# Spreading the last token group's block-sum splits over more slots, and moving the sums of the sixth output operand two sevenths ahead

## The chip, the cores and the metric

The kernel runs on one core of a Trainium2 chip. The metric is the device time of one execution in microseconds (us). TensorE (PE in the profile) multiplies matrices; VectorE (DVE), ScalarE (ACT) and GpSimd (POOL) do the elementwise work; SyncE (SP) issues the DMAs. Each engine works through its own instruction list in order, and waits on semaphores where an instruction needs another engine's result.

## What is computed

Causal attention over 4 batches of 12 heads (448 tokens, head size 64) gives `x` of 1792 tokens by 768. A gated feed-forward block follows:

```
rms  = sqrt(mean(x*x, axis=-1) + 1e-6)
xn   = x / rms * rms_g
g    = xn @ w_gate                       # 768 -> 1536
val  = xn @ w_val
out  = (g / (1 + exp(-g)) * val) @ w_out # 1536 -> 768
```

## The kernel before

**Precision.** Every float32 operand of the feed-forward products is split into a rounded high part (cast on ACT) and a low part (the difference, on DVE or POOL). A product is then three matmuls: high by high, high by low, low by high. So each operand costs one ACT cast, and behind it one subtraction on DVE or POOL.

**Stages.** The tokens form three groups: two of 512 and a last one of 768. The two groups of 512 go through the feed-forward in two passes over 36 weight units each (24 of gate and value, 12 of output weights; two units make one output block). A unit is three *slots* of six matmuls each; slot n of the second pass is the (n mod 3)-th part of unit (n-1)//3, so unit 33 takes slots 100 to 102. The attention work is interleaved with these passes. The third group's gate and value product, and its output product, come last. Both are done as a 2 by 2 block product with seven products in place of eight (a Winograd form), which needs sums and differences of blocks of both operands.

**The order around the first edit.** Everything is emitted in program order by one loop over slots, so every engine's queue holds the work in slot order. `split_w(s + 3)` (L384) is called in the last slot of each unit: it casts the weights of a unit three ahead on ACT (`w_h`, L389), and two slots later their low part `w_l` is subtracted, on DVE (L391) for odd units of the output weights and on POOL (L393, helper L102) for even ones. `ffn_part` (L421) emits the matmuls (L435 to L437; the third of each trio needs `w_l`) and, at the end of an output block, the eviction `ob` on DVE (L443), whose store SP issues three slots later (L445). The output block's PSUM bank is one of two with the tag "m". The loads of weight units (L361) and of the next stage's operands (`quad_load`, L560) are in SP's queue among these stores.

Once the attention is done (after slot 74 of the second pass), `x_steps` (L483) returns the list `todo`, and each later slot runs one entry of it. It scales the third group's `x` (L514), forms the block sums `t1`, `t2`, `t4` of three column chunks c on DVE (`sums`, L525, by `sub`, L523), and splits operand i, chunk c (`operand`, L535, which calls `split`, L472): one cast on ACT (L473), and a subtraction `cl`, on POOL for i in 0, 2 and 5, on DVE (L475) for 1, 3, 4 and 6. Twelve entries bring the scales and four early operands, three more the sums with one operand each; the last four entries hold all of operands 1, 3, 4 and 6, with (2, 2) and (5, 2) among them: slots 90, 91, 92 and 93.

**The order around the second edit.** The output product runs q = 0 to 20, with i, p = divmod(q, 3): seventh i, token chunk p (L939 to L950). After the 18 matmuls of step q the loop emits: the split of a weight operand of the next seventh (`wo_split`, cast `a_h` on ACT, `a_l` on DVE; six buffers), the load of one for the seventh after it (`wo_load`, SP, L661), the eviction (`out_result`, DVE, L717), for i = 0 sums and for i = 2 a difference on DVE, and then `h_operand(q + 4)` (L684), which casts the hidden operand `oh` on ACT and subtracts `ol` (on POOL for p = 0, else on DVE). There are four buffers of `oh` and `ol`, so the cast for step q + 4 can't start before step q's matmuls are through. For the sixth operand (i = 5, q + 4 = 15 to 17), `h_operand` first forms the difference `a12 - s2` on DVE (L692), and the cast behind it on ACT reads that. Each `out_product` of seventh i reads the three weight operands 3i to 3i + 2 in turn, six matmuls for each.

Of the kernel before, what the change touches and what calls it, by code (L numbers as in the profile page):

```python
# [14 lines left out]
ALU = mybir.AluOpType  # L15
# [46 lines left out]
def attention_ffn(ctx: ExitStack, tc: tile.TileContext, qk0, qk1, qk2, v, v2, w, g, out, out2):  # L62
# [7 lines left out]
    nc = tc.nc  # L70
# [22 lines left out]
    def bank(tag, bufs=1):  # L93


        return ps.tile([P, W], F32, tag=tag, name=tag + "_ps", bufs=bufs)
# [33 lines left out]
    def post(delay, fn):  # L130
        if delay <= 0:
            fn()
        else:
            later.setdefault(now[0] + delay, []).append(fn)
# [337 lines left out]
    def split(h, l, src, vec):  # L472
        nc.scalar.copy(h, src)  # L473
        if vec:
            nc.vector.tensor_tensor(l, src, f32(h), op=ALU.subtract)  # L475
        else:
            pool_op(l, src, ALU.subtract, f32(h))
# [5 lines left out]
    def x_steps():  # L483

        sm = side["sm"]
        rc = sm.tile([P, 6], F32, name="rc")
        dg = sm.tile([P, 2, HX], F32, tag="p2", name="dg").rearrange("p a (b c) -> p (a b) c", c=P)
        rb = {}

        def columns():  # L490
            ps = bank("t")[:, :6]
            for i in range(6):
                nc.tensor.matmul(ps[:, i: i + 1], acc[2, i // 3][:, P * (i % 3): P * (i % 3 + 1)],
                                 ones[:, :1], start=True, stop=True)
            nc.scalar.activation(rc, ps, AF.Sqrt, bias=eps, scale=1.0 / DM)
            post(1, lambda: nc.vector.reciprocal(rc, rc))

        def diagonal():
            for i in range(6):
                r = rc[:, i: i + 1]  # L500
                if i % 2:
                    nc.scalar.mul(dg[:, i], ident, r)
                else:
                    nc.gpsimd.tensor_scalar(dg[:, i], ident, r, 1.0, op0=ALU.mult, op1=ALU.mult)

        def spread():
            for j in (0, 1):
                rb[j] = bank("xy"[j])[:, :HX]
                nc.tensor.matmul(rb[j], ones, dg[:, 3 * j: 3 * j + 3].rearrange("p a b -> p (a b)"),
                                 start=True, stop=True)  # L510

        def scale(c, j):
            x = xr[2, c][:, HX * j: HX * (j + 1)]
            nc.vector.scalar_tensor_tensor(  # L514
                out=x, in0=x, scalar=g_sb[:, c: c + 1], in1=rb[j], op0=ALU.mult, op1=ALU.mult)

        tmp = {}

        def blk(k, j, c):
            return xq[c][:, k, HX * j: HX * (j + 1)]  # L520

        def sub(dst, a, b):
            nc.vector.tensor_tensor(dst, a, b, op=ALU.subtract)  # L523

        def sums(c):  # L525
            t12 = sm.tile([P, 2, HX], F32, tag=f"p{c}", name="t12")
            t1, t2 = t12[:, 0], t12[:, 1]
            t4 = sm.tile([P, HX], F32, tag=f"t4{c}", name="t4")
            sub(t1, blk(0, 1, c), blk(0, 0, c))
            sub(t2, blk(1, 1, c), t1)  # L530
            sub(blk(0, 1, c), blk(1, 1, c), blk(0, 1, c))
            sub(t4, blk(1, 0, c), t2)
            tmp[c] = t1, t2, t4

        def operand(i, c):  # L535
            if i not in xc:
                xc[i] = tuple(side["xc"].tile([P, 3, HX], F32R, name=f"{n}{i}") for n in ("ch", "cl"))
            t1, t2, t4 = tmp.get(c, (None,) * 3)
            src = (blk(0, 0, c), t2, blk(1, 0, c), t1, blk(0, 1, c), blk(1, 1, c), t4)[i]
            split(xc[i][0][:, c], xc[i][1][:, c], src, i not in (0, 2, 5))  # L540

        def scales(q):
            return [lambda j=j: scale(q, j) for j in (0, 1)]

        def op(i, c):
            return [lambda: operand(i, c)]

        todo = [[columns], [], [diagonal], [], [spread], [], scales(0), scales(3),
                scales(1) + op(0, 0), scales(4) + op(2, 0), scales(2) + op(5, 0), scales(5) + op(0, 1)]
        for c, i, k in ((0, 2, 1), (1, 5, 1), (2, 0, 2)):  # L550
            todo.append([lambda c=c: sums(c)] + op(i, k))
        for i, x in ((1, op(2, 2)), (3, op(5, 2)), (4, []), (6, [])):
            todo.append(op(i, 0) + op(i, 1) + op(i, 2) + x)
        return todo


# [1 line left out]
    f2 = {}  # L558
# [96 lines left out]
    def wo_load(n):  # L655
        if n >= 21:
            return
        i, sl = divmod(n, 3)
        t = wr_p.tile([P, 2, 3, P], F32, tag="w", name="w_o")
        for m in range(3):  # L660
            nc.sync.dma_start(out=t[:, :, m], in_=WSRC[i](m).rearrange("p (k m) -> p k m", m=P)[  # L661
                :, 2 * sl: 2 * sl + 2])
        wt["o", n] = t

    def wo_split(n):
        if n >= 21:
            return
        f2["o", n] = ring(8 * NF // 2 + n)
        split(*f2["o", n], wt["o", n].rearrange("p a b c -> p (a b c)"), True)

    def h_part(p):
        return [hid[:, 6 * k: 6 * k + 6, HX * e + P * p: HX * e + P * (p + 1)] for e in (0, 1) for k in (0, 1)]

    def h_sums(p):
        a11, _, a21, a22 = h_part(p)
        s1, s2 = f2["s", p] = [side["s"].tile([P, 6, P], F32, tag=n, name=n, bufs=3) for n in ("s1", "s2")]
        nc.vector.tensor_tensor(s1, a21, a22, op=ALU.add)
        nc.vector.tensor_tensor(s2, s1, a11, op=ALU.subtract)

    def h_difference(p):  # L680
        a11, _, a21, _ = h_part(p)
        nc.vector.tensor_tensor(a21, a11, a21, op=ALU.subtract)

    def h_operand(q):  # L684

        if q >= 21:
            return
        i, p = divmod(q, 3)
        a11, a12, a21, a22 = h_part(p)
        s1, s2 = f2.get(("s", p), (None, None))  # L690
        if i == 5:
            nc.vector.tensor_tensor(a12, a12, s2, op=ALU.subtract)  # L692
        src = (a11, a12, s2, s1, a21, a12, a22)[i]
        h, l = (side["ro" if q else "ro0"].tile([P, 6, P], F32R, tag=n, name=n) for n in ("oh", "ol"))
        split(h, l, src, p or not q)
        f2["h", q] = h, l

    def out_product(i, p):
        if i in (0, 4):
            f2["held", p] = bank("mmx"[p], 2 if p < 2 else 1)[:, :HX]  # L700
        ps = f2["held", p] if i in (0, 1, 4, 6) else bank("s", 2)[:, :HX]
        h = f2.pop(("h", 3 * i + p))
        for k in range(6):
            b = [t[:, HX * (k % 2): HX * (k % 2 + 1)] for t in f2["o", 3 * i + k // 2]]
            seven(ps, [t[:, k] for t in h], b, k == 0 and i not in (1, 6), k == 5)
        return ps

    def out_result(i, p, ps):

        g_ = side["g"]  # L710

        def add(n, u, bufs):
            t = g_.tile([P, HX], F32, tag=n, name=n, bufs=bufs)
            if u is None:
                nc.scalar.mul(t, ps, 0.5)
            else:
                nc.vector.scalar_tensor_tensor(out=t, in0=ps, scalar=0.5, in1=f2[u, p], op0=ALU.mult, op1=ALU.add)  # L717
            f2[n, p] = t
            return t

        if i in (0, 2, 3):
            add(*(("m1", None, 3), 0, ("u2", "m1", 3), ("u4", "u2", 3))[i])
            return
        c = add("c", {1: None, 4: "u4", 5: "u4", 6: "u2"}[i], 3)
        e, n = {1: (0, 0), 4: (1, 1), 5: (0, 1), 6: (1, 0)}[i]
        t0 = HX * e + P * p
        nc.sync.dma_start(out=out2[t0: t0 + P, HX * n: HX * (n + 1)], in_=c)
# [55 lines left out]
    with tc.manual_schedule():  # L783
# [32 lines left out]
        n = 0  # L816
        for t_, s, c in early:
            n = max(n, t_)
# [22 lines left out]
        todo = None  # L841
        for s in range(2 * NU):
# [9 lines left out]
            n = s + 6 - 2 * NU  # L852
# [5 lines left out]
            for k0 in (0, 2, 4):  # L858
# [3 lines left out]
                i = 3 * (s % NU) + k0 // 2 + 1  # L862
# [14 lines left out]
                n = 3 * (s - 2 * NU + 2) + k0 // 2  # L877
# [5 lines left out]
                if todo is None and done == len(steps) and i >= AT[1] + 1:  # L883
# [5 lines left out]
                    todo = x_steps()  # L889
# [14 lines left out]
        for v in range(NF):  # L904
            if v % 3 == 1 and v < 9:
                wo_sums(v // 3)
            for i in range(7):
                ps_ = quad_product(v, i)
                quad_result(v, i, ps_)
                if v + 1 < NF:  # L910
                    n = (0, 1, None, 2, None, 3, None)[i]
# [7 lines left out]
                if v + 2 < NF:  # L919
                    n = (None, None, 0, 1, None, 2, 3)[i]  # L920
# [13 lines left out]
        for q in range(1, 4):  # L934
            h_operand(q)
# [3 lines left out]
        for q in range(21):  # L939
            i, p = divmod(q, 3)  # L940
            ps_ = out_product(i, p)
            if i:
                wo_split(3 * (i + 1) + p)
                wo_load(3 * (i + 2) + p)
            out_result(i, p, ps_)
            if i == 0:
                h_sums(p)
            elif i == 2:
                h_difference(p)
            h_operand(q + 4)  # L950


# [46 lines left out]
```

## Time and profile before

| | us |
|---|---|
| median of three runs | 700.14 |
| lowest, highest | 699.67, 701.06 |
| the profiled execution | 702.16 |
| its span, first to last instruction | 700.40 |
| PE busy in it | 671.0 (96%) |
| DVE, ACT, POOL busy | 536.9, 371.6, 361.9 |

The profiled execution is 1.76 us longer than its span, and 2.02 us longer than the median of the runs. Times in the rows below count from the start of the span. A row of a timeline has the start in us, the duration in us, the engine, the line of the kernel, the operation, the tiles written and read, the shape, and a count; where an engine sat idle before the instruction, brackets give for how long and what ended the wait.

### The profile page before, as it was taken

What the parts mean: (1) busy time and instruction counts of PE and PEld (TensorE: products, weight loads), DVE (VectorE), ACT (ScalarE), POOL (GpSimd) and SP (SyncE); (2) the same over time, 40 slices, a digit from 0 to 9 for tenths busy, and PEclk for the clock granted to TensorE, in tenths of its full rate; (3) what the DMA queues carried; (4) which work ended last, traced back from release to release, by engine and by line L of the source; (5) the groups of instructions that cost most, each with busy time, mean ns of one, the idle gap of its engine ahead of it and who ended that gap; (6) DMA issues with size and microseconds to landing.
All of it is one profiled execution on the core that took longest, in us unless ns stands there. A gap on an engine that the chain in (4) does not pass through costs nothing. (4 is left out here: it accounts for less than half of the span.)

```text
span 700.4 us, 11930 instructions
## 1 busy us (share of the span) xinstructions
PE 671.0 (96%) x4106; PEld 550.9 (79%) x4106; DVE 536.9 (77%) x1029; ACT 371.6 (53%) x832; POOL 361.9 (52%) x313
## 2 busy tenths in 40 slices
PE   9878889999999999999999999997999999999997
PEld 6445667777777768777777777886999999999987
DVE  4976899989997667777687877396386868679973
ACT  6967876777685435436445353451433342445540
POOL 4988445545548534665776565552363536302220
PEclk9999999999999999999999999998999999999999
DMA  8746486868778547576767655333567576562541
GB/s 267 259 146 205 146 281 222 281 232 277 233 280 302 193 117 263 164 258 194 251 190 237 212 155 177 118 120 109 162 204 250 177 246 223 168 165 86 171 119 67
DMA packets 71355, 138.80 MB, mean 198 GB/s; under 512 B 7744, under 2 KB 39232, under 8 KB 71296
## 3 DMA queue, kind: packets, MB, share of 16 engines
q1 hardware_dynamic: 71296, 138.05, 60.3%
q8 instruction: 32, 0.52, 0.3%
q14 instruction: 27, 0.22, 0.1%
HBM read 104.21 MB, written 33.82 MB: 197 GB/s over the span
## 5 line engine op out<-in xcount | busy, mean ns | idle before, releaser
L208 POOL TENSOR_SCALAR sp<-sp,rs 128x384 f32<-128x384 f32 (+3 forms) x132 | 89.5, 696 | 95.8 <-DVE rs L212 84.8
L435 PE MATMUL m_ps<-xh,w_h 128*128 128x512 f32 x282 | 120.2, 426 | 3.7 <-DVE rs L212 3.7
L203 ACT ACTIVATE sp<-sp,nm 128x384 f32<-128x384 f32 (+3 forms) x168 | 87.2, 522 | 47.7 <-DVE nm L200 47.1
L437 PE MATMUL m_ps<-xh,w_l 128*128 128x512 f32 x282 | 111.3, 395 | 0.0
L436 PE MATMUL m_ps<-xl,w_h 128*128 128x512 f32 x282 | 111.1, 394 | 0.0
L102 POOL TENSOR_TENSOR a_l<-w_q,a_h 128x768 fp32r<-128x768 f32 x24 | 47.4, 1977 | 75.7 <-ACT a_h L473 75.6
L375 POOL TENSOR_SCALAR w<-w 128x768 f32<-128x768 f32 x36 | 46.5, 1292 | 53.1 <-ACT w_c L374 47.0
L274 PEld LDWEIGHTS a_ps<-pt,v_r 128*64 128x64 f32 (+1 forms) x864 | 40.7, 137 | 36.2 <-issue 11.1
L274 PE MATMUL a_ps<-pt,v_r 128*64 128x128 f32 (+2 forms) x864 | 57.1, 268 | 9.7 <-DVE pt L252 7.3
L435 PEld LDWEIGHTS m_ps<-xh,w_h 128*128 128x128 f32 x282 | 53.3, 189 | 16.1 <-issue 8.0
L437 PEld LDWEIGHTS m_ps<-xh,w_l 128*128 128x128 f32 x282 | 53.4, 189 | 12.1
L252 DVE COPY pt<-t_ps 128x384 f32<-128x384 f32 (+1 forms) x71 | 42.5, 598 | 26.6 <-PE t_ps L248 26.4
L437 PE MATMUL m_ps<-hh,w_l 128*128 128x512 f32 x144 | 57.8, 401 | 4.3 <-DVE w_l L391 3.9
L102 POOL TENSOR_TENSOR w_l<-w_r,w_h 128x768 fp32r<-128x768 f32 x30 | 59.2, 1979 | 3.6 <-ACT w_h L389 3.4
L436 PEld LDWEIGHTS m_ps<-xl,w_h 128*128 128x128 f32 x282 | 53.6, 190 | 7.8
L435 PE MATMUL m_ps<-hh,w_h 128*128 128x512 f32 x144 | 59.2, 411 | 0.0
L200 DVE CUSTOM_DVE_ANT_0 sp<-s_ps,mask 128x128 f32<-128x128 f32 (+3 forms) x136 | 49.8, 415 | 11.1 <-PE s_ps L191 9.3
L436 PE MATMUL m_ps<-hl,w_h 128*128 128x512 f32 x144 | 57.1, 397 | 0.0
L248 PE MATMUL t_ps<-ident,sp 128*128 128x128 f32 (+1 forms) x309 | 50.9, 277 | 1.4 <-ACT rms L335 0.8
L377 DVE SCALAR_TENSOR_TENSOR w<-w 128x768 int32<-128x768 int32 x36 | 45.4, 1261 | 8.0 <-POOL w L375 8.0
L248 PEld LDWEIGHTS t_ps<-ident,sp 128*128 128x128 f32 (+1 forms) x309 | 38.1, 138 | 16.7 <-POOL sp L208 2.6
L473 ACT CAST a_h<-w_q 128x768 fp32r<-128x768 f32 (+1 forms) x48 | 35.0, 753 | 24.9 <-PE m_ps L436 19.1
(176 smaller groups left out, 1702.1 us busy)
## 6 DMA issues: line engine op xcount, KB each, us to landing
w<-in_w SPq DMA_DIRECT2D x36, 768.0 KB, 5.9
w<-w_c SPq DMA_DIRECT2D x36, 384.0 KB, 2.7
w_r<-w SPq DMA_DIRECT2D x36, 384.0 KB, 4.5
qk_r<-in_qk SPq DMA_DIRECT2D x48, 256.0 KB, 4.0
qk_r<-in_qk SPq DMA_DIRECT2D x12, 512.0 KB, 5.6
v_r<-in_v SPq DMA_DIRECT2D x12, 448.0 KB, 5.1
v_r<-in_v SPq DMA_DIRECT2D x24, 192.0 KB, 3.4
wy<-w_r SPq DMA_DIRECT2D x24, 192.0 KB, 4.9
```

Source lines behind the costliest of these rows:

```text
L102: nc.gpsimd.tensor_tensor(out_, a, b, op=op)
L200: nc.vector.tensor_tensor_reduce(out=sp, in0=ps, in1=mk, scale=nsc, scalar=3.0e38, op0=ALU.add, op1=ALU.min, accum_out=nm)
L203: post(T["exp" if p >= ENDS[0] else "exp0"], lambda: nc.scalar.activation(sp, sp, AF.Exp, bias=nm, scale=-1.0, accum_out=sm))
L208: pr["norms"].append(lambda: nc.gpsimd.tensor_scalar(sp, sp, rs, 1.0, op0=ALU.mult, op1=ALU.mult))
L248: nc.tensor.transpose(ps[:kb, at: at + P], pr["sp"][e][:, o + kb * j: o + kb * (j + 1)], ident)
L252: nc.vector.tensor_copy(pt[:kb, :at], ps[:kb, :at])
L274: nc.tensor.matmul(av_ps[e * D: (e + 1) * D, p % 2, q0: q0 + n], raw_v[p][:kb, h, j, e, :], pr["pt", e][:kb, a0: a0 + n], start=(j == 0), ...
L375: (T["c1"], lambda: nc.gpsimd.tensor_scalar(hf_, hf_, 0.0, 1.0, op0=ALU.mult, op1=ALU.mult)),
L377: (T["c2" if s >= 5 else "c20"], lambda: nc.vector.scalar_tensor_tensor(out=lo, in0=lo, scalar=29, in1=hi, op0=ALU.logical_shift_right, op ...
L435: nc.tensor.matmul(ps, wh[:, k, :], mh, start=(first and k == ks[0]), stop=False)
L436: nc.tensor.matmul(ps, wh[:, k, :], ml, start=False, stop=False)
L437: nc.tensor.matmul(ps, wl[:, k, :], mh, start=False, stop=(last and k == 5))
```

## The change

The four last entries of `todo` become twelve: one (operand, chunk) to a slot, with (2, 2) put beside (1, 1) and (5, 2) beside (3, 1). They now take slots 90 to 101. The difference `a12 - s2` for the sixth operand leaves `h_operand` and goes to `h_difference`, which is now called at i = 2 and at i = 3: it is emitted at q = 9, 10 and 11 for p = 0, 1 and 2, instead of at q = 11, 12 and 13.

```diff
-        for i, x in ((1, op(2, 2)), (3, op(5, 2)), (4, []), (6, [])):
-            todo.append(op(i, 0) + op(i, 1) + op(i, 2) + x)
+        rest = op(2, 2) + op(5, 2)
+        for i in (1, 3, 4, 6):
+            for c in range(3):
+                todo.append(op(i, c) + (rest[:1] if c == 1 else []))
+                if c == 1:
+                    del rest[:1]
...
-    def h_difference(p):
-        a11, _, a21, _ = h_part(p)
-        nc.vector.tensor_tensor(a21, a11, a21, op=ALU.subtract)
+    def h_difference(n, p):
+        a11, a12, a21, _ = h_part(p)
+        if n == 0:
+            nc.vector.tensor_tensor(a21, a11, a21, op=ALU.subtract)
+        else:
+            nc.vector.tensor_tensor(a12, a12, f2["s", p][1], op=ALU.subtract)
...
-        if i == 5:
-            nc.vector.tensor_tensor(a12, a12, s2, op=ALU.subtract)
...
-            elif i == 2:
-                h_difference(p)
+            elif i in (2, 3):
+                h_difference(i - 2, p)
             h_operand(q + 4)
```

## Rows read from the trace of the kernel before

**Rows 1.** Waits of PE: who waited for whom, total us, times, longest us

```profile
PE m_ps L437 <- DVE w_l L391: 3.9, 1, 3.9
```

**Rows 2.** Timeline of PE: second pass, slots 99 and 100, and next stage's first product

```profile
475.86 0.39 PE L435 MATMUL m_ps<-hh,w_h 128*128 128x512 f32 x1
...
476.77 0.39 PE L436 MATMUL m_ps<-hl,w_h 128*128 128x512 f32 x1
481.04 0.79 PE L437 MATMUL m_ps<-hh,w_l 128*128 128x512 f32 x1 [3.88 <-DVE w_l L391]
...
495.72 0.33 PE L578 MATMUL m_ps<-ch,a_h 128*128 128x384 f32 x1
```

**Rows 3.** Windows: length; PE, PEld, DVE, ACT, POOL busy; PE clock; DMA share, GB/s

```profile
481.04:486.75 5.71, 5.71 (x14) 4.45 (x14) 1.41 (x2) 0.00 (x0) 0.00 (x0) 0.50 0.67 218
...
495.70:628.00 132.30, 131.47 (x756) 130.55 (x755) 96.28 (x139) 54.05 (x89) 56.45 (x28) 1.00 0.62 203
...
675.00:685.00 10.00, 8.36 (x47) 7.78 (x46) 9.02 (x11) 5.38 (x8) 1.96 (x1) 1.00 0.36 112
```

**Rows 4.** Timeline of DVE, slots 88 to 101 (by program order)

```profile
464.72 0.95 DVE L391 TENSOR_TENSOR w_l<-w_r,w_h 128x768 fp32r<-128x768 f32 x1
...
467.59 0.68 DVE L443 SCALAR_TENSOR_TENSOR ob<-m_ps,rms 128x512 f32<-128x512 f32 x1
...
470.90 2.20 DVE L475 TENSOR_TENSOR cl<-t,ch 128x384 fp32r<-128x384 f32 x1
473.02 0.55 DVE L475 TENSOR_TENSOR cl<-t,ch 128x384 fp32r<-128x384 f32 x1
...
480.04 0.94 DVE L391 TENSOR_TENSOR w_l<-w_r,w_h 128x768 fp32r<-128x768 f32 x1
```

**Rows 5.** Timeline of POOL, same stretch

```profile
467.77 1.02 POOL L102 TENSOR_TENSOR cl<-xq,ch 128x384 fp32r<-128x384 f32 x1 [6.32 <-ACT ch L473]
...
470.52 2.16 POOL L102 TENSOR_TENSOR w_l<-w_r,w_h 128x768 fp32r<-128x768 f32 x1
```

**Rows 6.** Timeline of ACT, same stretch: casts of operands (1,1) and (1,2)

```profile
463.90 0.51 ACT L473 CAST ch<-t 128x384 fp32r<-128x384 f32 x1 [1.48 <-DVE t L523]
466.77 0.51 ACT L473 CAST ch<-t 128x384 fp32r<-128x384 f32 x1 [2.35 <-DVE t L523]
```

**Rows 7.** Timeline of SP: loads of units 34, 35; landing times of all such loads

```profile
468.77 0.84 SPq L361 DMA_DIRECT2D w_r<-w  x2
...
DMA to landing us min/median/max: 3.0/3.6/4.3
```

**Rows 8.** Timeline of PE in the output product, step q = 15

```profile
675.73 0.33 PE L578 MATMUL s_ps<-a_h,oh 128*128 128x384 f32 x1
...
677.63 0.34 PE L578 MATMUL s_ps<-a_h,ol 128*128 128x384 f32 x1
678.93 0.45 PE L578 MATMUL s_ps<-a_h,oh 128*128 128x384 f32 x1 [0.96 <-ACT a_h L473]
680.06 0.44 PE L578 MATMUL s_ps<-a_l,oh 128*128 128x384 f32 x1 [0.68 <-DVE a_l L475]
680.34 0.34 PE L578 MATMUL s_ps<-a_h,ol 128*128 128x384 f32 x1
```

**Rows 9.** Timeline of DVE in the output product, steps q = 11 and 12

```profile
665.06 0.95 DVE L475 TENSOR_TENSOR a_l<-w_o,a_h 128x768 fp32r<-128x768 f32 x1
...
667.04 0.95 DVE L692 TENSOR_TENSOR hid<-hid,s 128x768 f32<-128x768 f32 x1
669.70 2.02 DVE L475 TENSOR_TENSOR a_l<-w_o,a_h 128x768 fp32r<-128x768 f32 x1 [1.72 <-ACT a_h L473]
```

**Rows 10.** Timeline of ACT in the output product: casts for q = 14 and 15

```profile
663.32 0.84 ACT L473 CAST oh<-hid 128x768 fp32r<-128x768 f32 x1 [1.55 <-issue]
...
668.10 0.83 ACT L473 CAST oh<-hid 128x768 fp32r<-128x768 f32 x1 [3.21 <-DVE hid L692]
```

**Rows 11.** Timeline of POOL in the output product: the subtraction for q = 15

```profile
669.07 1.85 POOL L102 TENSOR_TENSOR ol<-hid,oh 128x768 fp32r<-128x768 f32 x1 [9.23 <-ACT oh L473]
```

## The prediction, made before the changed kernel ran

> **What bounds the kernel now.** I read the page's shares first: PE is busy 96% of the span, so an edit pays only where PE stands still or runs slowly. The list of PE's waits comes next. One of them is by far the longest, 3.9 us for a `w_l` of DVE [rows 1]; the stage of the second edit has two short ones, for an `a_h` and the `a_l` behind it [rows 8]. Then PE's timeline around each.
>
> First gap. The trio of matmuls in slot 100 (unit 33) breaks off after its second one at 476.77; the third starts at 481.04 [rows 2]. Four matmuls before it went from 475.86 to 476.77, so the pace is 0.227 us, the third was due at 477.00, and 4.04 us are lost. The windows show what follows: from 481.04 to 486.75 the granted clock is 0.50 of full (1.2 GHz of 2.4) in 14 matmuls [rows 3], after PE had stood still for those four microseconds. From the third matmul of slot 100 to the first product of the next stage are 52 matmuls: at 0.227 us they end at 477.00 + 11.80 = 488.80, and the trace has that product at 495.72 [rows 2]. So this gap costs 6.92 us: 4.04 of standing still and 2.88 of slow clock.
>
> Why was `w_l` late? DVE ran it at 480.04 [rows 4], in its order behind all twelve subtractions `cl` of operands 1, 3, 4, 6, since these sit in slots 90 to 93 and this `w_l` is emitted at the end of slot 94. DVE began them only behind the eviction at 467.59 [rows 4], so at 468.3, and took 12 us for what is 0.55 us each when nothing is in the way. One took 2.20, from 470.90 to 473.10, beside a POOL subtraction that ran from 470.52 to 472.68 [rows 4, 5]: DVE ended 0.42 after POOL.
>
> Second gap. In q = 15 the thirteenth matmul was due 0.173 after 677.63, the fifteenth at 678.15, and it started at 680.34 [rows 8]: 2.19 us. The granted clock stays 1.00 here [rows 3]. The weights' cast was late because ACT stood idle ahead of the three casts of the sixth operand, 3.21 us ahead of the first, each time for DVE's difference L692 [rows 10, 9]; that difference in turn stands behind the eviction of the same step on DVE, and ACT's next weight cast behind the held cast.
>
> **The first edit, step by step.** No instruction is added or removed; the order changes on DVE, ACT and POOL, and with it when SP's stores and loads go.
> - *DVE, what stands ahead of unit 33's `w_l`.* At the end of slot 94, five of the twelve subtractions have been emitted instead of twelve. Seven move behind it.
> - *POOL comes earlier.* (2, 2) no longer waits behind (1, 2) on ACT. The cast (1, 1) ends at 463.90 + 0.51 [rows 6], (2, 2) at about 464.9, and POOL begins then, with DVE inside the `w_l` of 464.72 to 465.67 [rows 4]. POOL's 1.02 [rows 5] ends at 466.7, DVE's next sum 0.42 later at 467.1. Unit 32's `w_l` now follows at once on POOL, instead of at 470.52 [rows 5]: 1.85 us, to 468.9, and DVE's second sum ends at 469.3. In the trace it ended just ahead of 466.77, when ACT started on it [rows 6]. So the sums, and the eviction behind them, come 2.5 us later: the eviction ends at 468.27 + 2.5 = 470.8 [rows 4]. It frees a PSUM bank that slot 97 needs at 477.00 - 20 x 0.227 = 472.46: 1.7 us to spare.
> - *Unit 33's `w_l`.* From 470.8 three subtractions at 0.47 from start to start, then POOL's (5, 2) takes its turn for about 1.0 and 0.4 more, then one more and `w_l` with 0.95: it ends at 475.0, due at 477.00. The bounds: five at 0.55 from 468.27 give 472.0; five at 2.20 from 470.8 give 482.8, past the old end. I take 475.0, since only one POOL operation is left to meet these five. 2.0 us to spare.
> - *Units 34 and 35.* SP issues their loads behind the eviction's store, at 468.77 [rows 7], so now at 471.3 and 471.7; the landing took 4.3 at most, so 475.6 and 476.0. ACT waits for that ahead of seven casts (operands 4 and 6, and `w_h` of unit 35), which is a new wait, with DVE's `cl` of 4 and 6 and unit 35's `w_l` behind. Cast 0.84, POOL at most 2.16 [rows 5]: unit 34's `w_l` ends at 478.6, due at 477.00 + 18 x 0.227 = 481.09. Unit 35's `w_l` follows five `cl`s, the POOL operation and one more of the next stage: about 483.0, due at 477.00 + 36 x 0.227 = 485.17. 2.2 us to spare.
> - *The next stage.* SP's loads for it queue behind the store of the next eviction, which comes at 476 instead of 481. The stage is PE's alone from its start: 131.47 of 132.30 us busy at full clock [rows 3]. What feeds it hangs on PE's progress, so it moves up with it.
>
> Taken: the whole 6.92 us go. A smaller stall left over would cost its own length; the gaps of 1 us at full clock [rows 8, 3] show no slow clock behind them.
>
> **One rule weighed.** In the trace DVE's 2.20 ended 0.42 behind POOL's 2.16 [rows 4, 5], and in the output product DVE's 2.02 from 669.70 ended 0.80 behind POOL's 1.85 from 669.07 [rows 9, 11]: DVE waits for POOL to be through. The Trainium skill (SBUF — State Buffer, section Who interferes with whom) says that a DVE instruction with two SBUF inputs and a GpSimd instruction that reads SBUF contend, and that the first to issue holds the port while the other fully blocks. By that rule an earlier POOL start speaks against both edits; if the two merely shared, the eviction would keep its 468.27 and the sum would be the same 6.92 with 2.5 us more to spare. What it could cost is the first rival below. The trace agrees with the rule in both pairs.
>
> **The second edit.** Three differences of 0.95 us [rows 9] move from q = 11, 12, 13 to q = 9, 10, 11. No DMA moves with them.
> - *Gained.* The cast for q + 4 is now held only by its buffer, that is by the end of PE's step q. That end is 675.73 - 3 x 3.12 = 666.37 for q = 11 (18 matmuls at 0.173 are 3.12), and a cast started so at 663.32, for q = 10 [rows 8, 10]. So the casts run at 666.4, 669.5 and 672.6 instead of 668.10 and later; the last weight cast follows at about 673.4, and its `a_l` at about 675.6, behind two evictions and two `ol` on DVE. It was due at 677.63 + 2 x 0.173 = 677.98: 2.4 us to spare. The 2.19 us go.
> - *Paid.* At q = 9 and 10 the moved differences stand ahead of `ol` and `a_l` on DVE. The tightest is the `a_l` of q = 11: it started at 665.06 and now two differences later, at 666.96, to 667.91. It is read by the fourteenth matmul of q = 12, at 666.37 + 13 x 0.173 = 668.62: 0.7 us to spare. The loads that wait for its buffer land, at 4.3 us, long before their splits. Cost taken: nothing, bound 1.4 us (first rival).
>
> **The sum.** 6.92 + 2.19 = 9.1 us. The profiled execution of 702.16 (span 700.40, 1.76 around it) would take 693.1; the median of the runs, 2.02 lower, 700.14 - 9.1 = 691.0.
>
> **Rivals.**
> - *POOL gets ahead of DVE in q = 12's weights.* The cast for q = 15 would start at 663.32 + 3.12 = 666.44 and end at 667.27, POOL 0.14 behind it as in 668.10 to 669.07 [rows 10, 11], so at 667.41. If `a_l` isn't under way by then (it is due to start at 666.96, 0.45 sooner), it ends 0.80 behind POOL, at 667.41 + 1.85 + 0.80 = 670.06, and PE loses 1.4 us: 692.4. For it: half a microsecond decides. Against: both hang on PE's end of step 11 and 8, with nothing of the DMA between.
> - *A shorter wait stays in the second pass.* The sums are 2.5 us later, and three margins of about 2 us stand between the estimate and PE. If another POOL operation falls in, a wait of 1 to 3 us remains, 692 to 694. For it: twelve `cl`s were on average at 1.0, not 0.55. Against: POOL has one operation left for the first five.
> - *The second edit only shifts its own wait.* DVE is busy 9.02 of 10 us there [rows 3]; if it is DVE's load and not ACT's waiting that made `a_l` late, nothing is gained: 693.2. Against: ACT's wait for L692 [rows 10] held DVE too, 1.72 us ahead of one `a_l` [rows 9].
> - *The first edit doesn't relieve `w_l`*, since the work emitted ahead is what holds DVE (the upper bound above, 482.8): 700.14 - 2.19 = 697.9. Against: the seven that go behind it ran after the one of 473.02, up to 480.04 [rows 4].
> - *The stall moves to unit 35, and the kernel is slower.* ACT's cast of unit 34 waits for a load behind a later store, and unit 35's `w_l` hangs on it through five casts. From 485.17 on each microsecond counts, with 2.9 of slow clock behind a long stall as in the first gap. It takes back all 9.1 us at 6.2 us of stall, a `w_l` ending at 491.4 instead of 483.0; at 9 us of stall it is 703. For it: a new wait with a queue behind it. Against: that load would have to land some 12 us after its issue where none took over 4.3 [rows 7].
>
> **How the numbers follow.** Forecast 0.65 (691.0, of its own 689.8 to 692.0: the runs lie within 0.5 us below and 0.9 above their median). First rival 0.10 (692.4), second 0.10 (692 to 694), third 0.06 (693.2), fourth 0.05 (697.9), last 0.04 (700 to 703). The range goes from 689.6 to 694.0 and leaves out the last two. A change of 0.2% (1.4 us) is about what runs of this kernel can tell: faster is all but the last, 0.96; of the last 0.01 within it and 0.03 slower.
>
> **What would show it.** In PE's waits the line of 3.9 us is gone, with no window of clock 0.50 near 480, and the next stage's first product comes near 488.8. Unit 33's `w_l` ends near 475 on DVE, and the eviction ahead of it near 470.8. In the output product ACT no longer waits for a difference of `hid`, and PE has no gap in q = 15. Wrong would be: a wait of PE at slots 97, 100, 103 or 106, one in q = 12 for `a_l`, or a next stage that starts sooner but ends no sooner.

## The result, and the profile after

The changed kernel takes 691.76 us in the median of four runs (689.29 to 693.80); the kernel before, run beside it, 700.08. The ratio is 0.9878, with a 95% interval of 0.984 to 0.9915. Two later rounds, with more runs of the kernel before, gave 0.987 (0.9845 to 0.9895) and 0.9868 (0.9839 to 0.9897). The forecast was 691.0, and the range went from 689.6 to 694.0.

PE's waits in the profile after, from 430 us on (the same view as rows 1: who waited for whom, total us, times, longest us). The line of 3.9 us [rows 1] and the two of step 15 [rows 8] are gone. The first line isn't in the first profile of before; the second profile of before, in the table below, has it too, with 1.3 us:

```profile
PE y_ps L582 <- DVE c L616: 1.1, 2, 0.7
PE m_ps L582 <- ACT m L605: 0.8, 1, 0.8
PE m_ps L582 <- DVE ol L475: 0.2, 1, 0.2
```

The windows after, around where the long gap was (columns as in rows 3). PE is busy throughout and the clock is full, where rows 3 have 0.50:

```profile
477.00:481.04 4.04, 4.04 (x19) 3.37 (x18) 4.04 (x5) 1.75 (x3) 1.89 (x1) 1.00 0.18 54
481.04:486.75 5.71, 5.71 (x26) 4.71 (x26) 1.59 (x3) 0.84 (x1) 1.85 (x1) 1.00 0.69 208
```

To compare profiles, four marks cut the span into stages. Here they are in PE's timeline after (the first is the column sums of the last group, slot 75; the second the first product of the gate and value stage; the third the first output product), and in DVE's (the last eviction):

```profile
439.36 1.39 PE L493 MATMUL t_ps<-ones,acc 128*128 128x1 f32 x12
...
486.98 0.33 PE L582 MATMUL m_ps<-ch,a_h 128*128 128x384 f32 x1
...
621.33 0.33 PE L582 MATMUL m_ps<-a_h,oh 128*128 128x384 f32 x1
```

```profile
687.60 0.56 DVE L722 SCALAR_TENSOR_TENSOR c<-x_ps,u 128x384 f32<-128x384 f32 x1 [2.57 <-PE x_ps L582]
```

The table gives the lengths between these marks for every profile of this study, in us, and the median of that kernel's runs in its round. From the last eviction to the end it is 3.5 to 3.6 in all of them.

| kernel | median | up to the column sums | from there to gate and value | gate and value | output product |
|---|---|---|---|---|---|
| before | 700.08 | 441.08 | 54.64 | 132.62 | 68.50 |
| before, second profile | 700.43 | 440.04 | 53.47 | 134.17 | 68.55 |
| changed | 691.76 | 439.36 | 47.62 | 134.35 | 66.27 |
| changed, second (again) | 691.94 | 439.81 | 47.63 | 134.13 | 66.24 |
| changed, third (again2) | 692.45 | 440.54 | 47.62 | 133.73 | 66.26 |
| part1 | 693.64 | 437.14 | 47.62 | 132.92 | 70.02 |
| part2 | 697.72 | 437.70 | 53.48 | 133.83 | 66.33 |
| w33 | 693.33 | 437.48 | 48.95 | 135.92 | 66.30 |
| flip | 692.12 | 440.73 | 47.62 | 134.04 | 66.33 |
| flip2 | 692.05 | 438.78 | 47.63 | 133.80 | 67.21 |
| late_sums | 692.14 | 437.98 | 47.62 | 133.70 | 66.24 |
| early_loads | 690.04 | 439.29 | 47.62 | 132.26 | 66.25 |
| early_loads2 | 690.42 | 438.84 | 47.62 | 132.28 | 66.25 |

Between the first two profiles of before and after, the span goes from 700.40 to 691.1: 1.72 less up to the column sums, 7.02 less up to the gate and value stage, 1.73 more in that stage, and 2.23 less in the output product. The second and the fourth are the two edits. The first is chance: no edit touches that part, and over all profiles it lies anywhere between 437.1 and 441.1. Single runs of one kernel lie some 4 us apart (the changed kernel's first four 4.5, the kernel before 7.4 in one round, by one run of 705.58), so the stage columns decide more than the medians. The third was the question of the experiments.

### The profile page after: what moved, and what is told of

The parts are those of the page before. It is cut to its first block, busy times and chain, and to the rows that moved or that the text cites. A ratio compares the mean times of both kernels' runs of the same rounds, so it can differ in the third digit from the quotient of the medians.

```text
span 691.1 us, 11932 instructions
## 1 busy us (share of the span) xinstructions
PE 669.5 (97%) x4106; PEld 550.4 (80%) x4106; DVE 536.2 (78%) x1029; ACT 371.7 (54%) x832; POOL 362.5 (52%) x313
## 5 line engine op out<-in xcount | busy, mean ns | idle before, releaser
L102 POOL TENSOR_TENSOR a_l<-w_q,a_h 128x768 fp32r<-128x768 f32 x24 | 47.6, 1984 | 64.7 <-ACT a_h L473 63.2
L437 PE MATMUL m_ps<-hh,w_l 128*128 128x512 f32 x144 | 56.4, 391 | 0.1
L377 DVE SCALAR_TENSOR_TENSOR w<-w 128x768 int32<-128x768 int32 x36 | 47.0, 1305 | 7.9 <-POOL w L375 7.9
L379 DVE SCALAR_TENSOR_TENSOR w_c<-w_c,w 128x768 int32<-128x768 int32 x36 | 46.4, 1290 | 0.6
```

The lines of the kernel that those rows point to most:

```text
L102: nc.gpsimd.tensor_tensor(out_, a, b, op=op)
L377: (T["c2" if s >= 5 else "c20"], lambda: nc.vector.scalar_tensor_tensor(out=lo, in0=lo, scalar=29, in1=hi, op0=ALU.logical_shift_right, op ...
L437: nc.tensor.matmul(ps, wl[:, k, :], mh, start=False, stop=(last and k == 5))
```

## The experiments

**The two edits apart.** `part1` is the changed kernel without its second edit, `part2` without its first; the changed kernel ran beside them.

> The changed kernel once more, beside the two halves. Theory: the two edits remove 6.9 and 2.2 us, and the gate and value stage of the last group gave 1.7 us back in the one profile of it, because two loads for the block sums of the output weights landed later there (7.5 us instead of 5.9). If that is chance, the median comes near 700.1 - 9.1 = 691.0, and a second profile has the stage at 132.6 to 134.4 us, from its first product to the first output product. If the stage is slower for a reason in the change (POOL or DVE in another order, loads on each other's heels), it has 134.4 us again and the median is near 692.5.

> The first edit alone (the splits one a slot; the differences for the sixth operand stay where they were). Theory: the wait of 3.9 us for unit 33's weights and the slow clock behind it go, 6.9 us: 693.2, with the two short waits in step 15 of the output product as before (2.2 us). Rival, that the whole gain is the second edit's and the first one's shifts only the stall: 698 to 700. If the stage after the first edit gives back 1.7 us for a reason in this edit: 694.9.

> The second edit alone (the differences two sevenths sooner; the splits in four slots as before). Theory: ACT no longer waits for the differences, the gap of 2.2 us in step 15 goes, the stall of 3.9 us and its slow clock stay: 697.9. Rival, that DVE's load and not ACT's waiting made the weights late: 700.1. The gate and value stage as before, 132.6 us, if what slowed it in the changed kernel is in the first edit.

Measured: 691.94 (ratio 0.987), 693.64 (0.990, 0.9877 to 0.9923) and 697.72 (0.995, 0.9931 to 0.9969). In the stage columns each edit does its own piece: the first takes the second column to 47.6, the second the last column to 66.3. The rivals that one of them only shifts its wait have fallen.

Two sizes differ from the expectation, both by the clock. With the first edit alone, the output product took 70.02 instead of 68.5. Its two waits in step 15 are those of before, but in this profile the clock fell behind them. PE's timeline and windows of `part1`:

```profile
668.20 0.44 PE L582 MATMUL s_ps<-a_h,oh 128*128 128x384 f32 x1 [0.96 <-ACT a_h L473]
669.33 0.57 PE L582 MATMUL s_ps<-a_l,oh 128*128 128x384 f32 x1 [0.68 <-DVE a_l L475]
669.70 0.52 PE L582 MATMUL s_ps<-a_h,ol 128*128 128x384 f32 x1
```

```profile
667.00:669.00 2.00, 0.69 (x3) 0.19 (x1) 1.55 (x2) 2.00 (x4) 0.00 (x0) 1.00 0.72 192
669.00:671.00 2.00, 1.67 (x6) 1.67 (x7) 2.00 (x3) 0.67 (x2) 1.95 (x1) 0.62 0.24 82
671.00:673.00 2.00, 2.00 (x8) 2.00 (x7) 2.00 (x3) 1.52 (x2) 0.00 (x0) 0.52 0.10 34
673.00:675.00 2.00, 2.00 (x13) 2.00 (x12) 0.98 (x2) 0.00 (x0) 0.00 (x0) 1.00 0.27 98
```

A matmul takes 0.52 there instead of 0.33, until about 673, and that costs 1.5 us. With the second edit alone the long wait of 3.9 us is as before, but the slow clock ended sooner. Windows of `part2`, where the stall ended near 478:

```profile
478.00:480.00 2.00, 2.00 (x6) 1.54 (x6) 1.06 (x2) 0.00 (x0) 0.00 (x0) 0.50 0.51 159
480.00:482.00 2.00, 2.00 (x8) 1.63 (x7) 0.00 (x0) 0.00 (x0) 0.00 (x0) 0.72 0.94 287
482.00:484.00 2.00, 2.00 (x11) 1.64 (x10) 0.78 (x2) 0.84 (x1) 0.00 (x0) 1.00 0.45 177
```

The stage took 53.48 instead of 54.64, so the slow clock cost 1.8 us (53.48 - 47.62 less 4.04 of standing still), where the same sum gives 3.0 for the first profile of before (2.88 in the prediction).

**The kernel before, once more.**

> The kernel before once more, for a second profile. If the stages are steady: 54.6 us from the third group's column sums to the first product of the gate and value stage (the long wait and its slow clock among them), 132.6 for that stage, 68.5 for the output product. If the slow clock behind a wait differs from run to run, as it did with each of the two edits alone (1.8 us instead of 2.9 behind the long wait; 1.5 instead of none behind the two short ones), the first is between 53.4 and 54.7 and the last 68.5 or 70.0. What comes ahead of the column sums, which neither edit touches, should vary by some 4 us between runs: 437 to 441 us.

Measured: 53.47, 134.17, 68.55. Windows of this profile, where the long wait ended at 479.99:

```profile
480.00:482.00 2.00, 2.00 (x7) 1.63 (x8) 1.40 (x2) 0.00 (x0) 0.00 (x0) 0.75 0.32 116
482.00:484.00 2.00, 2.00 (x6) 1.52 (x5) 0.00 (x0) 0.00 (x0) 0.00 (x0) 0.50 0.99 278
484.00:486.00 2.00, 2.00 (x9) 1.66 (x8) 0.45 (x1) 0.64 (x1) 0.00 (x0) 0.89 0.63 229
```

So the same long wait has a slow clock of 1.8 us behind it in one profile and 3.0 in another, by the same sum; and the gate and value stage of the kernel *before* can be as long as the changed kernel's. What the changed kernel lost there in the first pair of profiles needs no cause in the change. That the change adds nothing at all there isn't shown: its three profiles have 133.7 to 134.4, `part1` 132.92, and the two of before 132.62 and 134.17.

**One instruction instead of twelve slots.** `w33` has the second edit, leaves the splits in their four slots, and moves one subtraction:

```diff
-                post(T["wl" if s > 1 else "wl0"], lambda: nc.vector.tensor_tensor(l, t, f32(h), op=ALU.subtract))
+                post(0 if s == NU + 33 else T["wl" if s > 1 else "wl0"], lambda: nc.vector.tensor_tensor(l, t, f32(h), op=ALU.subtract))
```

> The second edit alone, and in place of the first one a single instruction moved: unit 33's low part of the weights is emitted at once with its cast, in slot 93, ahead of the three subtractions of operand 6; the splits stay in four slots. Theory, that all the first edit is worth is this one instruction's place in DVE's order: nine subtractions stand ahead of it instead of twelve (five in the changed kernel), so it ends near 478.0 on the scale of the kernel before, due at 477.00, and PE waits about 1.0 us instead of 3.9. If a wait of 1 us leaves the clock alone, the time is the changed kernel's 691.9 plus 1.0 to 1.2, 693; with a slow clock behind it as after the long wait, 694.5 to 696. Rival, that spreading itself matters (ACT's and POOL's bursts): 697.7 as with the second edit alone, or a new wait at unit 35.

Measured: 693.33 (0.9903, 0.9882 to 0.9923), and 48.95 in the second column. DVE's and PE's timelines:

```profile
472.01 1.48 DVE L475 TENSOR_TENSOR cl<-xq,ch 128x384 fp32r<-128x384 f32 x3
473.41 0.94 DVE L391 TENSOR_TENSOR w_l<-w_r,w_h 128x768 fp32r<-128x768 f32 x1
474.28 3.12 DVE L475 TENSOR_TENSOR cl<-t,ch 128x384 fp32r<-128x384 f32 x3
```

```profile
474.41 0.50 PE L437 MATMUL m_ps<-hh,w_l 128*128 128x512 f32 x1 [0.91 <-DVE w_l L391]
```

The `w_l` ends at 474.35; with the column sums 3.60 us sooner than in the profile of before that is 477.95 on its scale, where 478.0 was forecast. PE waits 0.91, the clock stays full, and the stage is 1.33 longer than with the whole edit. So the place of this one instruction in DVE's order is worth 54.64 - 48.95 = 5.7 of the 7.0 us, or 4.5 by the other profiles of the long wait; the rest goes when the spread brings it in front of four more. Whether a still earlier place without the spread would do as much was not tried. That the gate and value stage took 135.92 here goes with another wait: DVE's first `u` of that stage (L606) stood 4.65 us for the last output store of the pass before it, and PE 1.1 us behind DVE. Five other profiles have this wait of DVE with 3.35 to 4.05 us, and there PE doesn't wait behind it. It was not followed further.

**What holds the gate and value stage up.** In the changed kernel DVE waited there for the loads of the block sums of the output weights (`wo_sums`, L629 before), and PE behind it. DVE's and PE's timelines after:

```profile
506.66 0.96 DVE L642 TENSOR_TENSOR wq<-wq 128x768 f32<-128x768 f32 x1 [1.67 <-DMA wq<-w]
507.53 0.55 DVE L616 TENSOR_TENSOR c<-u,y_ps 128x384 f32<-128x384 f32 x1
```

```profile
508.14 0.44 PE L582 MATMUL y_ps<-ch,a_h 128*128 128x384 f32 x1 [0.68 <-DVE c L616]
```

The first try was to emit these sums two steps later:

```diff
-        post(4, lambda: sums(0))
-        post(8, lambda: sums(1))
-        post(12, store)
+        post(6, lambda: sums(0))
+        post(10, lambda: sums(1))
+        post(14, store)
```

> The changed kernel, with the block sums of the output weights (and the stores behind them) emitted two steps, some 3.1 us, later behind their loads: 6, 10 and 14 steps instead of 4, 8 and 12. Theory, that late landings of these loads hold DVE (1.7 and 1.4 us in the profile of the changed kernel) and through it the evictions that PE waits for (0.7 and 0.4 us, with what follows from them 1.7): DVE no longer waits there, the stage takes 132.6 us or less, and the median is 1.0 to 1.7 us under the changed kernel's, near 690. Rival, that the stage's loss comes from POOL and DVE blocking each other: the same time as the changed kernel.

Measured: 692.14, and 133.70 for the stage: no gain. DVE's wait for the loads is gone, and PE's for `c`; in their place PE waits longer for ACT, in three places where one was. PE's waits of `late_sums`:

```profile
PE m_ps L582 <- ACT m L605: 1.7, 3, 0.7
PE m_ps L582 <- DVE ol L475: 0.2, 1, 0.2
```

The two longer ones of these three waits, 0.72 us each, are new. About 5.8 us ahead of each of them DVE stands beside POOL: a DVE instruction (L620) takes 1.86 us there, where the changed kernel has 1.27 and 0.88 at the same two places. POOL came to the subtraction that runs beside it straight from one of the sums that the try had moved. DVE's and POOL's timelines of `late_sums` at the first place:

```profile
516.61 1.86 DVE L620 SCALAR_TENSOR_TENSOR t<-t,c 128x384 f32<-128x384 f32 x1 [0.59 <-ACT t L619]
```

```profile
514.41 1.85 POOL L102 TENSOR_TENSOR wq<-wq 128x768 f32<-128x768 f32 x1 [1.77 <-DVE wq L645]
516.22 1.84 POOL L102 TENSOR_TENSOR a_l<-w_q,a_h 128x768 fp32r<-128x768 f32 x1
```

Behind this DVE instruction come DVE's `c`, ACT and PE; that the blocking alone makes the two new waits was not tried. So the rival's mechanism, that DVE and POOL hold each other up, is seen in this try; but the try moved the sums themselves, and so it says nothing on the loads alone. For that reason the second try leaves the sums at their steps and issues the loads seven steps sooner:

```diff
-            if v % 3 == 1 and v < 9:
+            if v % 3 == 0 and v < 9:
                 wo_sums(v // 3)
...
-        post(4, lambda: sums(0))
-        post(8, lambda: sums(1))
-        post(12, store)
+        post(11, lambda: sums(0))
+        post(15, lambda: sums(1))
+        post(19, store)
```

> The changed kernel, with the loads for the block sums of the output weights issued seven steps (11 us) earlier, and the sums and stores at the same steps as before, so that DVE's and POOL's order of work stays as it was. Theory, that late landings of these loads are what cost the gate and value stage its 1.0 to 1.7 us: DVE has no wait for them, PE's waits for the evictions behind it (0.7 and 0.4 us in one profile, 0.2 and 0.8 in the other) go without others in their place, the stage takes 132.6 to 133.0 us and the median is near 690.7. Rival, that DVE and POOL hold each other up in that stage whatever the loads do, as the variant with later sums suggests: 134 us and 691.9.

Measured: 690.04 (689.31 to 690.76), 132.26 for the stage. It was repeated beside the changed kernel on one chip:

> The loads for the block sums seven steps earlier, again, beside the changed kernel on the same chip. If the gain of the first try (690.0 beside 691.9 in another round) is the loads', the median is 1.0 to 2.0 us under the changed kernel's, the stage takes 132.3 us again, and DVE has no wait for the loads. If it was the rest of the program that varies, the two medians are within 0.7 us and the stage is anywhere from 132.3 to 134.4.

> The changed kernel a third time, to stand beside the next one on the same chip: a median near 691.9, with 47.6 us up to the gate and value stage, 132.3 to 134.4 for that stage by how late the loads for the block sums land, and 66.25 for the output product.

Measured: 690.42 (689.09 to 690.53) beside 692.45 (690.77 to 693.47); the two sets of runs don't overlap. The ratio to the kernel before is 0.984 (0.9809 to 0.9872) beside 0.9868. The stage took 132.28 beside 133.73. DVE's waits in this stage have no line for these loads any more, where the changed kernel's third profile has this one:

```profile
DVE wq L642 <- DMA wq<-w: 2.6, 2, 1.4
```

and of PE's waits only ACT's 0.8 is left in the stage. So the loads were the cause of the waits for `c`; the first try, which moved the sums as well, put others in their place. This version beats both kernels: the one before by 1.4 to 1.6%, the changed one by 2.0 us on one chip. Of these 2.0 us the stage has 1.45 in the two profiles of that round; the rest is no more than the medians vary by.

**The narrow place in step 12.** The prediction's first rival had POOL's subtraction for step 15 come ahead of the `a_l` that step 12 reads last. `flip` forms the third difference one step earlier, so that this `a_l` starts later:

```diff
-            elif i in (2, 3):
-                h_difference(i - 2, p)
+            elif i == 2:
+                h_difference(0, p)
+            elif i == 3:
+                for c in ((0,), (1, 2), ())[p]:
+                    h_difference(1, c)
```

> The changed kernel, with the third of the moved differences one step earlier: two of them at step 10 of the output product and none at step 11. This puts 0.87 us more ahead of the low part of the weights that step 12 reads last, which in the changed kernel started 0.69 us ahead of POOL's subtraction. Theory (the first rival of the prediction, brought about on purpose): POOL starts first, DVE waits for it and ends 0.8 behind it, and PE stands 1.4 us in step 12: the output product takes 1.4 us more than 66.25, 67.7, and the median is 693.3, or up to 1.5 more if the clock falls. If POOL and DVE only shared the port, or the margin is larger than the trace says: no wait, 691.9.

Measured: 692.12, and 66.33 for the output product; PE doesn't wait in step 12. DVE's and POOL's timelines of `flip`:

```profile
661.58 0.94 DVE L475 TENSOR_TENSOR a_l<-w_o,a_h 128x768 fp32r<-128x768 f32 x1
```

```profile
661.41 2.82 POOL L102 TENSOR_TENSOR ol<-hid,oh 128x768 fp32r<-128x768 f32 x1 [7.58 <-ACT oh L473]
```

POOL's row starts 0.17 ahead of the `a_l`, and yet the `a_l` takes its usual 0.94 and POOL the longer time. `flip2` adds one subtraction more at step 10 (s2 of the first chunk, to the same values):

```diff
+                if p == 1:
+                    a11 = h_part(0)[0]
+                    s1, s2 = f2["s", 0]
+                    nc.vector.tensor_tensor(s2, s1, a11, op=ALU.subtract)
```

> The variant with the third difference at step 10, and one more subtraction of the same size on DVE at that step (a block sum formed a second time, to the same values): 0.87 us more ahead of the low part that step 12 reads last. In the variant before it started 0.17 us behind POOL's request and still went first, POOL waiting, and ended at the moment PE wanted it. Theory, that the port goes to one of the two for a whole instruction: POOL now comes between, the low part ends 0.8 behind POOL, about 2.5 us late, and the output product takes 68.7 us instead of 66.3; the median is 694.3 or, with a slow clock behind the wait, up to 696. Rival, that DVE keeps the port as long as its queue is full: POOL waits on, the low part is 0.7 to 0.9 us late, the output product takes 67.1 and the median is 692.8.

Measured: 692.05, and 67.21 for the output product: 0.94 more than in the changed kernel, about what the rival said (67.1). PE has one new wait, 0.66 us. The median doesn't show the 0.94, beside 692.45 for the changed kernel in that round; it is read from the stage column. DVE's, POOL's and PE's timelines of `flip2`:

```profile
659.39 0.94 DVE L475 TENSOR_TENSOR ol<-hid,oh 128x768 fp32r<-128x768 f32 x1
660.26 0.94 DVE L475 TENSOR_TENSOR a_l<-w_o,a_h 128x768 fp32r<-128x768 f32 x1
661.13 0.54 DVE L722 SCALAR_TENSOR_TENSOR u<-s_ps,u 128x384 f32<-128x384 f32 x1
661.60 2.12 DVE L475 TENSOR_TENSOR a_l<-w_o,a_h 128x768 fp32r<-128x768 f32 x1
```

```profile
659.22 3.69 POOL L102 TENSOR_TENSOR ol<-hid,oh 128x768 fp32r<-128x768 f32 x1 [7.57 <-ACT oh L473]
```

```profile
661.26 0.44 PE L582 MATMUL m_ps<-a_l,oh 128*128 128x384 f32 x1 [0.66 <-DVE a_l L475]
```

POOL asked at 659.22, if the start of its row is taken for that. DVE started two more subtractions behind that, at 659.39 and 660.26, each at its usual 0.94. POOL, which takes 1.85 alone [rows 11], was through at 662.91, so it began about 661.06, when DVE came to an eviction that reads PSUM; and only the subtraction behind that waited for POOL (2.12).

## Why the prediction was right

**How close, and how much of that was luck.** The forecast of the profiled execution, 693.1, met 692.92, but only since two differences that the forecast doesn't have cancelled: 1.72 less up to the column sums, 1.73 more in the gate and value stage. The runs of the changed kernel lie 4.5 us apart, where the prediction took 0.5 below and 0.9 above the median from three runs, so a median within 0.8 us is luck in part. What was right are the two pieces in the stage columns.

**The first edit** was right in its mechanism and, against the profile that it was worked out from, in its size: 7.02 us by the stage column, 6.92 forecast. Its steps can be held against the timelines after, which run 1.72 us ahead of the profile of before at the column sums. DVE's:

```profile
463.00 0.95 DVE L391 TENSOR_TENSOR w_l<-w_r,w_h 128x768 fp32r<-128x768 f32 x1
463.87 1.37 DVE L523 TENSOR_TENSOR t<-xq 128x384 f32<-128x384 f32 x1
465.28 2.08 DVE L523 TENSOR_TENSOR t<-xq,t 128x384 f32<-128x384 f32 x1
...
468.22 0.68 DVE L443 SCALAR_TENSOR_TENSOR ob<-m_ps,rms 128x512 f32<-128x512 f32 x1
468.82 3.24 DVE L475 TENSOR_TENSOR cl<-t,ch 128x384 fp32r<-128x384 f32 x5
471.98 0.95 DVE L391 TENSOR_TENSOR w_l<-w_r,w_h 128x768 fp32r<-128x768 f32 x1
...
478.10 2.60 DVE L391 TENSOR_TENSOR w_l<-w_r,w_h 128x768 fp32r<-128x768 f32 x1
```

and POOL's and ACT's:

```profile
463.19 1.64 POOL L102 TENSOR_TENSOR cl<-xq,ch 128x384 fp32r<-128x384 f32 x1 [3.46 <-ACT ch L473]
464.79 2.15 POOL L102 TENSOR_TENSOR w_l<-w_r,w_h 128x768 fp32r<-128x768 f32 x1
```

```profile
473.12 0.84 ACT L389 CAST w_h<-w_r 128x768 fp32r<-128x768 f32 x1 [2.82 <-DMA w_r<-w]
```

| step | forecast, scale of before | measured + 1.72 |
|---|---|---|
| POOL begins (2, 2) | 464.9 | 464.91 |
| eviction ends | 470.8 | 470.62 |
| unit 33's `w_l` ends | 475.0 | 474.65 |
| unit 35's `w_l` ends | 483.0 | 482.42 |

POOL's two operations, now side by side in time with the last sums (1.37 and 2.08 us instead of 0.55), took from the eviction what the prediction said, and none of the margins was used up. The new wait for unit 34's load is there, 2.82 us on ACT, and what it holds comes in time. `w33` shows that most of the gain is the place of unit 33's `w_l`.

**The term that varies** is the slow clock. The sum took 2.88 us for it from one profile as if it were a fixed price. Behind the same wait of 3.9 us it cost 1.8 in two other profiles, and behind the two short waits of step 15 it cost nothing in two profiles and 1.5 in a third. So the prediction's step that a smaller stall would cost its own length, read from the full clock behind the short gaps in one profile, doesn't hold in `part1`. By the stage columns the first edit is worth 5.9 to 7.0 us and the second 2.2 to 3.8, by how the clock falls; the sum of 9.1 lies inside, and the three rounds have 8.2 to 9.4.

**The second edit**: 2.23 measured, 2.19 forecast. The casts for steps 15 to 17 are held by the buffers alone, as said; ACT's timeline after:

```profile
659.38 0.84 ACT L473 CAST oh<-hid 128x768 fp32r<-128x768 f32 x1 [1.55 <-issue]
...
662.50 0.84 ACT L473 CAST oh<-hid 128x768 fp32r<-128x768 f32 x1 [1.55 <-POOL ol L102]
...
665.62 0.84 ACT L473 CAST oh<-hid 128x768 fp32r<-128x768 f32 x1 [1.55 <-issue]
```

With the first output product 7.01 us sooner than in the profile of before, these are 666.39, 669.51 and 672.63 on its scale, where 666.4, 669.5 and 672.6 were forecast. They come 3.12 us apart, a step of PE's, where ACT had stood idle 3.21 us ahead of the first of them for the difference [rows 10].

**The next stage "moves up with it"**: this step was too simple. It did move up, but PE isn't the only thing that paces it. The profile of before showed 131.47 of 132.30 us busy [rows 3], and I took that for the stage's nature; it was one good instance of a stage that takes 132.6 to 134.4 in the kernels that differ by the two edits alone, much of it by when some loads land.

**The rivals.** The stall didn't move to unit 35, no shorter wait stayed in the second pass, and the second edit didn't shift its own wait. The first rival didn't come about, and its reasoning was wrong in one step: that POOL, once it asks first, takes the port before DVE's next subtraction. In `flip` its row starts 0.17 us ahead of the `a_l` and DVE went first, and in `flip2` DVE went first twice. With 0.87 us more of DVE's work PE doesn't wait at all, and with 1.74 it loses 0.94, not 1.4. The section of the Trainium skill that the prediction weighed (SBUF — State Buffer, Who interferes with whom) says that issue order decides who blocks. The sums after agree (POOL asks at 463.19 and DVE's sum from 463.87 waits for it); `flip2` doesn't, with POOL's 3.69 us. The measurement decides: while one is blocked, which of them is next isn't settled by whose row starts first.

## What to carry to other kernels

Where an engine's order is written out slot by slot, a burst of work that no one needs yet is dear only by what it stands in front of: look for the one instruction behind it that PE waits for, and price its place, then see whether one move does as much as the whole spread. Check the load of a moved piece apart from its work: here late loads were cured by issuing them sooner, not by using them later. And a stage that looks fully busy in one profile may be one good instance; a second profile of the kernel before costs little and tells how much of a difference is chance.

## What the runs showed of the hardware that was not expected

The price of a stall has a part that changes from run to run: behind the same wait of 3.9 us the clock stood at 1.2 GHz for a cost of 1.8 us in two profiles and 3.0 in a third, and behind two waits of 0.96 and 0.68 us it fell in one profile of three. What decides it was not tried.

POOL can stand blocked through several DVE instructions: 1.84 us, two subtractions long, in `flip2`, until DVE came to an instruction with one operand in PSUM. In the second pass it got in between two subtractions (463.19 after). Why it was let in there and not here stays open.
